# Fourteen rotating weight tiles of an attention and mixer kernel begin 8 to 112 bytes later

## The chip, the cores and the metric

The kernel runs on one core of a Trainium2 chip. The metric is the device time of one execution in microseconds (us), the median of several runs; smaller is better. The engines are named as the profile names them: PE is TensorE (matmul), PEld its weight load, DVE is VectorE, ACT is ScalarE, POOL is GpSimd and SP is SyncE, whose queue carries the DMA transfers here.

## The reference, cut to what matters

```python
def reference(**kwargs):
    attn_out = _attn_ref(q, k, v, n_global, n_local)   # (2, 8, 768, 64)
    x = attn_out.transpose(0, 2, 1, 3).reshape(2, 768, 512)
    # first mixer
    h = np.maximum(x.transpose(0, 2, 1) @ w_tok1, 0.0) @ w_tok2
    u = x + h.transpose(0, 2, 1)
    x = u + np.maximum(u @ w_ch1, 0.0) @ w_ch2         # 512 -> 1536 -> 512
    # second mixer
    theta = x @ w_theta
    zr, zi = x * np.cos(theta), x * np.sin(theta)
    y = np.einsum('ts,bsd->btd', w_tok_r, zr) + np.einsum('ts,bsd->btd', w_tok_i, zi)
    u = x + y
    return u + np.maximum(u @ w_ch, 0.0)
```

Attention keeps a band of 96 keys and 8 global ones. The weights come as float64 and are used in that precision as far as two float32 numbers carry it.

## The kernel before, in words

Each large float32 matmul is split in three: an operand is held as a high and a low part in the type F32R, and `mm3` (line 93) issues high x high, high x low and low x high into one PSUM accumulator. A *split weight tile* holds the high and the low part of a 128 x 512 block: 512 words (2048 bytes) each, one behind the other in each partition, 4096 bytes in all.

The weights are prepared by *jobs*: SP loads the raw 64-bit words into a staging tile `raw`, ACT and DVE and POOL convert them (lines 136 to 146, in tiles `cvt` and `cvs`), then ACT writes the high part into the split weight tile (`job_high`, line 154) and DVE reads it and writes the low part (`job_low`, line 157). A job advances one phase at each `tick`, and ticks stand by hand between the matmuls. No DMA writes a split weight tile.

Where split weight tiles live decides what the change touches:

- Pool `we` has 4 tiles (`EARLY`): the first mixer's channel pieces k = 0 and 1 (two halves each), later `wri0` to `wri3`.
- Pool `ws` has 14 tiles that rotate: the channel pieces of k = 2 to 8 (`wc2_0` to `wc8_1`, made by `channel_piece`), and later, by turns, `wri4` to `wri17` of the second mixer (made by `token`).
- One large tile holds the channel pieces of k = 9 to 11, and later the last weight `wch`; the weight `w_theta` sits in two tiles of the x pool.

A channel piece's half 0 (of `w_ch1`) is the **weight** (stationary) operand of the matmuls `gp<-xh,wc` and `gp<-xl,wc`, 128 words of a part at a time; the moving operand there is the activation. Half 1 (of `w_ch2`) is the **moving** operand of `h<-wc,g`, 512 columns each. The tiles `wri` are the moving operand of `y<-wri,s` and `y<-wri,z`: two of each three with 512 columns, the third (numbers 2, 5, 8, 11, 14, 17) with 256.

The order is written by hand: the attention with the token mixing between (to about 125 us of the span), then `channel_mix`, which for each of the two batches and each k first issues the 24 matmuls of `up` for the next step and then the 18 of `down` for this one, then `PhaseB.run`, which mixes with the 18 `wri` tiles for each batch, then the last matmuls `v`. A value matmul of the attention (line 403) multiplies by 65 columns of a tile `v` or `a`, whose rows lie apart by an odd-looking width:

```python
VW = 2 * D + 2
            po[:, j * OW : j * OW + D + 1], lhsT=at, rhs=v[:, j * (D + 1) : (j + 1) * (D + 1)],
```

With D = 64, block n of such a tile begins 130 n words behind the tile's start, and head j's columns 65 j words further. Every tile of the program begins at a multiple of 32 bytes, and each of the split weight tiles, and of the activations that are matmul operands with them, at 32 bytes past a multiple of 64.

Of the kernel before, what the change touches and what calls it, by code (L numbers as in the profile page):

```python
# [15 lines left out]
F32 = mybir.dt.float32  # L16
# [9 lines left out]
P = 128  # L26
NS = S // P
NHP = H // 2
E = H * D
# [51 lines left out]
class Build:  # L81
# [680 lines left out]
    def token_jobs(self):  # L762
# [16 lines left out]
        for i in range(self.EARLY):  # L779
            self.channel_job(*divmod(i, 2))  # L780

    def channel_piece(self, pool, k, half):
        w = pool.tile([P, 2, E], F32, name="wc%d_%d" % (k, half), tag="w")
        self.set_channel(k, half, w)

    def set_channel(self, k, half, w):
        if half == 0:
# [92 lines left out]
    def moe_jobs(self, ws, w12p):  # L880

        dram = self.dram
        self.start_jobs()
        self.wc_job, self.wr_job = {}, {}
        self.wt, self.wr, self.wch = [], [], []
        self.ws, self.w12p = ws, w12p

        for i in range(2 * NF):
            self.wc_job[divmod(i, 2)] = 0 if i < self.EARLY else self.channel_job(*divmod(i, 2))

        def theta(d):
            if d == 0:
                self.s0 = self.xs.tile([P, NS, E], F32, name="s0", tag="xs")
                self.s1 = self.xs.tile([P, NS, E], F32, name="s1", tag="xs")
                for i in range(NE):
                    t = self.s0 if i < 3 else self.s1
                    j = 2 * (i % 3)
                    self.wt.append((t[:, j], t[:, j + 1]))
            return self.wt[d]

        for d in range(NE):
            self.wt_job = self.add_job(
                dram["w_theta"][d * P : (d + 1) * P, :], lambda d=d: theta(d), 1
            )

        def token(i):
            pool = self.early if i < self.EARLY else ws
            w = pool.tile([P, 2, E], F32, name="wri%d" % i, tag="w")
            self.wr.append((w[:, 0], w[:, 1]))
            return self.wr[i]  # L910

        for i in range(3 * NS):
            s, j = divmod(i, 3)
            self.wr_job[s] = self.add_job(
                dram["w_tok"][s * P : (s + 1) * P, 2 * j * E : 2 * (j + 1) * E],
                lambda i=i: token(i),
                2 + i // 2,
            )

        def last(d):  # L920
            if d == 0:
                w = w12p.tile([P, NS, 2, E], F32, name="wch", tag="w")
                self.wch = [(w[:, i, 0], w[:, i, 1]) for i in range(NE)]
                self.wch_rest = w[:, NE:NS].rearrange("p a l e -> p (a l) e")
            return self.wch[d]

        for d in range(NE):
            self.wch_job = self.add_job(
                dram["w_ch"][d * P : (d + 1) * P, :], lambda d=d: last(d), 1 + NF
            )  # L930
# [354 lines left out]
```

## Time and profile before

| | us |
|---|---|
| median of 3 runs (503.14 to 503.77) | 503.31 |
| the profiled execution, its own time | 503.15 |
| its span, from the first to the last instruction | 501.4 |

| engine | busy us | share of the span | instructions |
|---|---|---|---|
| PE | 495.9 | 99% | 2908 |
| PEld | 421.6 | 84% | 2908 |
| DVE | 309.1 | 62% | 671 |
| ACT | 236.2 | 47% | 458 |
| POOL | 163.4 | 33% | 175 |

A matmul's duration in the profile overlaps that of the next, since matmuls are pipelined. What one costs in a row of them is the distance from its start to the next one's start, called its *step* below. A row of the timeline merges like neighbours (x18) and gives their first start and the time to the last end.

### The profile page before, as it was taken

What the parts mean: (1) busy time and instruction counts of PE and PEld (TensorE: products, weight loads), DVE (VectorE), ACT (ScalarE), POOL (GpSimd) and SP (SyncE); (2) the same over time, 40 slices, a digit from 0 to 9 for tenths busy, and PEclk for the clock granted to TensorE, in tenths of its full rate; (3) what the DMA queues carried; (4) which work ended last, traced back from release to release, by engine and by line L of the source; (5) the groups of instructions that cost most, each with busy time, mean ns of one, the idle gap of its engine ahead of it and who ended that gap; (6) DMA issues with size and microseconds to landing.
All of it is one profiled execution on the core that took longest, in us unless ns stands there. A gap on an engine that the chain in (4) does not pass through costs nothing.

```text
span 501.4 us, 7724 instructions
## 1 busy us (share of the span) xinstructions
PE 495.9 (99%) x2908; PEld 421.6 (84%) x2908; DVE 309.1 (62%) x671; ACT 236.2 (47%) x458; POOL 163.4 (33%) x175
## 2 busy tenths in 40 slices
PE   9999999999999999999999999999999999999997
PEld 4888878887888888888888888888888889888896
DVE  4788878736877575216473565377888886351342
ACT  6888778714755554112554544435555334232010
POOL 7455444410342333001332151144555543333000
PEclk9999999999999999999999999999999999999999
DMA  6797764202453443002443121222210000000012
GB/s 199 209 269 237 227 214 143 85 3 59 152 147 125 135 126 104 0 1 59 118 129 117 42 61 65 85 84 76 73 62 1 1 1 0 22 22 22 21 66 103
DMA packets 30013, 45.93 MB, mean 92 GB/s; under 512 B 1936, under 2 KB 20880, under 8 KB 29968
## 3 DMA queue, kind: packets, MB, share of 16 engines
q1 hardware_dynamic: 29968, 45.36, 29.9%
q8 instruction: 25, 0.41, 0.3%
q14 instruction: 20, 0.16, 0.1%
HBM read 42.21 MB, written 3.15 MB: 90 GB/s over the span
## 4 chain that ended last, share of the span: by engine, by line
PE 98%; ACT 1%; DVE 1%; issue 0%; DVEq 0%; ACTq 0%
PE gp L93 20%; PE y L93 20%; PE h L93 20%; PE th L93 7%; PE v L93 7%; PE o L403 6%; PE mm L93 6%; PE s L434 5%; PE t L481 5%; PE warm L327 1%; PE ut L759 1%; DVE xl L709 0%; ACT xh L703 0%; PE xt_2p L759 0%; PE xt_0p L759 0%; PE xt_1p L759 0%
## 5 line engine op out<-in xcount | busy, mean ns | idle before, releaser
L146 POOL TENSOR_TENSOR cvt<-cvt,cvs 128x512 int32<-128x512 int32 (+1 forms) x57 | 75.8, 1330 | 218.3 <-DVE cvt L145 173.1
L93 PE MATMUL h<-wc,g 128*128 128x512 f32 x432 | 102.5, 391 | 0.0
L93 PE MATMUL gp<-xh,wc 128*128 128x512 f32 (+1 forms) x384 | 98.1, 337 | 0.1
L93 PEld LDWEIGHTS h<-wc,g 128*128 128x128 f32 x432 | 79.7, 188 | 15.7
L705 DVE SCALAR_TENSOR_TENSOR g<-gp,g 128x512 fp32r<-128x512 f32 (+1 forms) x48 | 26.8, 557 | 84.7 <-ACT g L703 84.6
L93 PEld LDWEIGHTS gp<-xh,wc 128*128 128x128 f32 x384 | 67.5, 189 | 8.6 <-DVE xl L709 0.3
L93 PE MATMUL gp<-xl,wc 128*128 128x512 f32 (+1 forms) x192 | 64.5, 336 | 0.0
L703 ACT ACTIVATE g<-gp 128x512 fp32r<-128x512 f32 (+1 forms) x48 | 23.5, 490 | 71.3 <-PE gp L93 71.3
L93 PE MATMUL y<-wri,z 128*128 128x256 f32 (+1 forms) x288 | 52.2, 336 | 0.0
L93 PE MATMUL y<-wri,s 128*128 128x256 f32 (+1 forms) x288 | 52.1, 336 | 0.0
L93 PEld LDWEIGHTS y<-wri,s 128*128 128x128 f32 x288 | 44.9, 190 | 6.0
L93 PEld LDWEIGHTS y<-wri,z 128*128 128x128 f32 x288 | 44.9, 190 | 6.0
L481 PE MATMUL t<-ident,e 128*128 128x128 f32 x176 | 48.1, 285 | 0.4 <-ACT at L493 0.4
L142 DVE SCALAR_TENSOR_TENSOR cvs<-cvt,cvs 128x512 int32<-128x512 int32 (+1 forms) x57 | 44.4, 779 | 0.0
L93 PEld LDWEIGHTS gp<-xl,wc 128*128 128x128 f32 x192 | 36.4, 189 | 4.6
L481 PEld LDWEIGHTS t<-ident,e 128*128 128x128 f32 x176 | 31.6, 184 | 8.2 <-issue 2.3
L136 ACT ACTIVATE cvt<-raw 128x512 f32<-128x512 f32 (+1 forms) x57 | 37.3, 655 | 2.0 <-issue 2.0
L447 DVE CUSTOM_DVE_ANT_0 e<-s,base 128x256 f32<-128x256 f32 (+1 forms) x96 | 32.8, 398 | 8.6 <-PE s L434 8.5
L137 ACT ACTIVATE cvs<-raw 128x512 int32<-128x512 uint16 (+1 forms) x57 | 37.4, 657 | 0.0
L1075 ACT ACTIVATE w<-w 128x512 f32<-128x512 f32 x12 | 7.6, 634 | 57.1 <-DVE w L1072 57.1
L403 PE MATMUL o<-v,at 128*128 128x65 f32 x192 | 32.3, 252 | 0.0
L403 PEld LDWEIGHTS o<-v,at 128*128 128x128 f32 x192 | 29.8, 196 | 0.0
(136 smaller groups left out, 813.9 us busy)
## 6 DMA issues: line engine op xcount, KB each, us to landing
raw<-w_ch SPq DMA_DIRECT2D x28, 512.0 KB, 3.7
raw<-w_tok SPq DMA_DIRECT2D x21, 512.0 KB, 3.6
k<-k SPq DMA_DIRECT2D x7, 480.0 KB, 6.0
v<-v SPq DMA_DIRECT2D x8, 384.0 KB, 3.8
out<-o SPq DMA_DIRECT2D x11, 256.0 KB, 2.0
q<-q SPq DMA_DIRECT2D x7, 384.0 KB, 5.3
raw<-w_theta SPq DMA_DIRECT2D x4, 512.0 KB, 3.7
a<-v SPq DMA_DIRECT2D x8, 240.0 KB, 4.7
```

Of the source, the lines that this page charges most:

```text
L93: self.nc.tensor.matmul(out, lhsT=a, rhs=b, start=first and i == 0, stop=last and i == n - 1)
L136: nc.scalar.activation(out=f(t), in_=f(top), func=AF.Copy, scale=2.0**-111)
L137: nc.scalar.activation(out=s, in_=nxt, func=AF.Copy, scale=2.0**-13)
L142: nc.vector.scalar_tensor_tensor(out=s, in0=t, scalar=-(1 << 31), in1=s, op0=ALU.bitwise_and, op1=ALU.bitwise_or)
L146: nc.gpsimd.tensor_tensor(out=t, in0=t, in1=s, op=ALU.add)
L403: self.nc.tensor.matmul(po[:, j * OW : j * OW + D + 1], lhsT=at, rhs=v[:, j * (D + 1) : (j + 1) * (D + 1)], start=first, stop=last,)
L434: nc.tensor.matmul(ps[j][:, ii, c0:], lhsT=t["q"][pj, i * P : (i + 1) * P], rhs=kf[pj, i * KW - P + c0 : i * KW + P], start=True, stop=True,)
L447: nc.vector.tensor_tensor_reduce(out=e, in0=ps[j][:, ii, c0:], in1=self.base[2 * hp + j][min(i, 1)], op0=ALU.add, op1=ALU.min, scale=-SCAL ...
L481: nc.tensor.transpose(pt[:, ii, c, :], e[j][:, ii, c * P : (c + 1) * P], self.ident)
L703: nc.scalar.activation(out=hi, in_=ps, func=AF.Relu if relu else AF.Copy)
L705: nc.vector.scalar_tensor_tensor(out=lo, in0=ps, scalar=0.0, in1=f(hi), op0=ALU.max, op1=ALU.subtract)
L1075: nc.scalar.activation(out=a, in_=t, func=AF.Abs)
```

## The change

The 14 tiles of pool `ws` grow by 32 words (128 bytes, 4096 to 4224 bytes a tile), and the 4096 bytes of high and low part begin 4, 12, 20, 28, 2, 10 or 6 words behind the tile's start, by turns. For the channel pieces the turn is that of k - 2, so both halves of one k have one offset; for the tiles `wri` it is that of the number less 4. The tiles of `we` and the large tile of k = 9 to 11 keep their places.

```diff
+    SHIFT = (4, 12, 20, 28, 2, 10, 6)
+
+    def split_tile(self, pool, name, n):
+        if pool is self.early:
+            return pool.tile([P, 2, E], F32, name=name, tag="w")
+        w = pool.tile([P, 2 * E + 32], F32, name=name, tag="w")
+        c0 = self.SHIFT[n % len(self.SHIFT)]
+        return w[:, c0 : c0 + 2 * E].rearrange("p (l e) -> p l e", l=2)
+
     def channel_piece(self, pool, k, half):
-        w = pool.tile([P, 2, E], F32, name="wc%d_%d" % (k, half), tag="w")
-        self.set_channel(k, half, w)
+        self.set_channel(k, half, self.split_tile(pool, "wc%d_%d" % (k, half), k - 2))
...
         def token(i):
             pool = self.early if i < self.EARLY else ws
-            w = pool.tile([P, 2, E], F32, name="wri%d" % i, tag="w")
+            w = self.split_tile(pool, "wri%d" % i, i - self.EARLY)
             self.wr.append((w[:, 0], w[:, 1]))
             return self.wr[i]
```

| offset in words | 4 | 12 | 20 | 28 | 2 | 10 | 6 |
|---|---|---|---|---|---|---|---|
| bytes | 16 | 48 | 80 | 112 | 8 | 40 | 24 |
| bytes past a multiple of 32 | 16 | 16 | 16 | 16 | 8 | 8 | 24 |
| channel pieces of k | 2 | 3 | 4 | 5 | 6 | 7 | 8 |
| `wri` | 4, 11 | 5, 12 | 6, 13 | 7, 14 | 8, 15 | 9, 16 | 10, 17 |

On every engine the instructions stand in the order they had, with the shapes and the waits they had. The pool is 14 x 128 = 1792 bytes larger in each partition, so the pools that are placed next to it (`g`, `xt`, `tb`) begin 1792 bytes lower, still at multiples of 32 bytes. All loops, matmuls, copies and transfers are the same in number.

## Rows read from the trace of the kernel before

**Rows 1.** The page: span, busy time by engine, and the chain that ended last.

```profile
span 501.4 us, 7724 instructions
...
PE 495.9 (99%) x2908; PEld 421.6 (84%) x2908; DVE 309.1 (62%) x671; ACT 236.2 (47%) x458; POOL 163.4 (33%) x175
...
PE 98%; ACT 1%; DVE 1%; issue 0%; DVEq 0%; ACTq 0%
```

**Rows 2.** Who PE waited for in the whole span: total us, times, longest.

```profile
PE warm L327 <- DVE halfpi L225: 1.2, 1, 1.2
PE mm L93 <- ACT xh L703: 0.5, 1, 0.5
PE t L481 <- ACT at L493: 0.4, 1, 0.4
```

**Rows 3.** Cores: span and mean granted clock.

```profile
core 0: 501.4 us, clock 1.000
```

**Rows 4.** Tiles wc and wri: count, duration ns min/median/max, first and last start.

```profile
L93 PEld LDWEIGHTS gp<-xh,wc x384: 186/188/192, 125.3 to 324.6; 128*128 128x128 f32 x192
L93 PEld LDWEIGHTS gp<-xl,wc x192: 187/188/192, 125.4 to 324.5; 128*128 128x128 f32 x192
L93 PE MATMUL h<-wc,g x432: 387/389/487, 135.1 to 332.8; 128*128 128x512 f32 x144
L93 PE MATMUL y<-wri,s x288: 277/338/398, 333.0 to 467.1; 128*128 128x256 f32 x72, 128*128 128x512 f32 x72
L93 PE MATMUL y<-wri,z x288: 277/338/398, 344.5 to 478.2; 128*128 128x256 f32 x72, 128*128 128x512 f32 x72
L154 ACT ACTIVATE wc<-cvt x24: 619/632/637, 81.6 to 200.5; 128x512 fp32r<-128x512 f32 x24
L157 DVE SCALAR_TENSOR_TENSOR wc<-cvt,wc x24: 681/682/1740, 84.2 to 202.2; 128x512 fp32r<-128x512 f32 x24
L154 ACT ACTIVATE wri<-cvt x18: 615/626/635, 255.3 to 371.7; 128x512 fp32r<-128x512 f32 x18
L157 DVE SCALAR_TENSOR_TENSOR wri<-cvt,wri x18: 681/684/1153, 260.0 to 381.1; 128x512 fp32r<-128x512 f32 x18
```

**Rows 5.** Timeline of PE in `channel_mix` and `PhaseB`: start us, us, what, count.

```profile
143.39 4.27 PE L93 MATMUL h<-wc,g 128*128 128x512 f32 x18
147.50 0.39 PE L93 MATMUL gp<-xh,wc 128*128 128x512 f32 x1
...
385.16 5.60 PE L93 MATMUL y<-wri,s 128*128 128x512 f32 x24
390.60 3.04 PE L93 MATMUL y<-wri,z 128*128 128x256 f32 x24
393.48 0.60 PE L759 MATMUL xt_2p<-ident,x 128*128 128x128 f32 x4
```

**Rows 6.** Timeline of PE among value matmuls of batch 1, first head pair, blocks 4 and 5.

```profile
60.22 0.33 PE L403 MATMUL o<-v,at 128*128 128x65 f32 x2
60.39 0.28 PE L481 MATMUL t<-ident,e 128*128 128x128 f32 x1
60.50 0.33 PE L403 MATMUL o<-a,at 128*128 128x65 f32 x2
60.67 0.28 PE L481 MATMUL t<-ident,e 128*128 128x128 f32 x1
60.79 0.33 PE L403 MATMUL o<-v,at 128*128 128x65 f32 x2
60.96 0.28 PE L481 MATMUL t<-ident,e 128*128 128x128 f32 x1
61.08 0.34 PE L403 MATMUL o<-a,at 128*128 128x65 f32 x2
61.25 0.28 PE L481 MATMUL t<-ident,e 128*128 128x128 f32 x1
```

**Rows 7.** Timeline of DVE and PE: writes of `wc2_0`, of `wri17`, first read of `wc2_0`.

```profile
130.23 0.68 DVE L157 SCALAR_TENSOR_TENSOR wc<-cvt,wc 128x512 fp32r<-128x512 f32 x1
...
139.24 0.39 PE L93 MATMUL gp<-xh,wc 128*128 128x512 f32 x1
...
381.09 0.68 DVE L157 SCALAR_TENSOR_TENSOR wri<-cvt,wri 128x512 fp32r<-128x512 f32 x1
```

## The prediction

> **What bounds the kernel now.** I read the page first. PE is busy for 495.9 of 501.4 us and the chain that ended last is PE for 98% [rows 1]. Then the waits of PE: three in the whole span, 2.1 us together, none of them for a tile that the change touches [rows 2]. [...] So the time is the sum of the steps of the matmuls, and an edit counts only if it makes a step of PE longer or shorter, or makes PE wait where it doesn't wait now.
>
> The steps come from the timeline. 18 matmuls `h` run from 143.39 to the next one's start at 147.50: 4.11 / 18 = 228 ns for 512 columns. 24 of `y` with 512 columns take 390.60 - 385.16 = 5.44 us, 227 ns each; 24 with 256 columns take 393.48 - 390.60 = 2.88 us, 120 ns each [rows 5]. Between 256 and 512 columns a step grows by 107 ns, so a column costs 107 / 256 = 0.42 ns, and a fixed part of 120 - 107 = 13 ns is left. I use both as prices below.
>
> **The change part by part.** No instruction is added, removed or moved; three kinds of access get a start that is no multiple of 32 bytes.
>
> 1. *Moving reads by PE.* Half 1 of k = 2 to 8 is 7 of 12 channel pieces: 432 x 7 / 12 = 252 matmuls `h` with 512 columns. Of the 576 matmuls `y`, tile numbers 4 to 17 serve: nine tiles with 512 columns, 24 matmuls each, 216; five with 256 columns (5, 8, 11, 14, 17), 48 each, 240 [rows 4]. That is 708 reads on the path, with nothing to hide a longer one.
>
> 2. *Weight loads by PE.* Half 0 of k = 2 to 8: 576 x 7 / 12 = 336 loads [rows 4], half ahead of 512-column matmuls and 168 ahead of 256-column ones. A load lasts 188 ns but lies beside the matmuls before it; a load is behind only where the step is shortest, at 120 ns.
>
> 3. *Writes by ACT and reads and writes by DVE.* 14 channel pieces and 14 `wri` tiles: 28 writes of about 0.63 us on ACT, 28 of 0.68 us on DVE [rows 4]. What hides them is how early they are: the low part of `wc2_0` is done at 130.91 and read at about 139.0, just ahead of the matmul at 139.24; that of `wri17` is done at 381.77 and read by the 256-column run at 390.60 [rows 5, 7]. These are the shortest leads that I found among the 28, 8 us each. If every such write took twice as long, a piece would be late by 1.3 us of its 8. The next instructions on ACT and DVE would be late by that too, the evacuations of `gp` among them, but PE has the whole of a next `up`, 4 us, before it reads their result. So nothing.
>
> 4. *The other tiles.* Pools `g`, `xt` and `tb` slide by 1792 bytes, a multiple of 64, so their starts keep their class. Nothing.
>
> What does a read by PE from such a start cost? No F32R matmul of before has one, so I bound it. The nearest rows are the value matmuls, whose moving operand begins at many places, since a block is 130 words and a head 65. Taken from the code, block 4 of `v` for the first head begins at a multiple of 32 bytes (520 words), block 4 of `a` too, block 5 of `v` 8 bytes past one (650 words), and block 3 of `a` for the second head 28 bytes past one (455 words). Their rows begin at 60.22, 60.50, 60.79 and 61.08, and the next instruction starts 0.17 us later each time [rows 6]. Aligned or not, the same to the 10 ns of the display. That says a start off 32 bytes costs no restart of its own. It leaves one thing open: 260 bytes touch nine 32-byte pieces from any of these starts, and these plain f32 matmuls take their columns more slowly (two instructions and 170 ns for 65 columns). A 2048-byte row touches 64 pieces when it begins on one and 65 when it doesn't.
>
> Bounds: below, nothing, or a gain if the present starts are the slow ones, at most the whole fixed part, 708 x 13 ns = 9.2 us. Above, one 32-byte piece more per moving read, 8 columns x 0.42 = 3.3 ns, 708 x 3.3 = 2.4 us; with one piece in 16 more on the weight loads, 188 / 16 = 12 ns, all of it visible at the 168 short steps, 2.0 us more; at the extreme the fixed part paid twice, +9.2 us. The value matmuls are the nearest row, and by them I take 0.
>
> The rows show 0 for starts of 8 and 28 bytes past a multiple of 32 [rows 6]. [...]
>
> The sum is 0, against the profiled 503.15 us (501.4 of span and 1.75 around it); the median of the runs stands 0.16 above it. I predict 503.3 us. What a measurement of this kernel can tell from no change is about 0.2%, 1.0 us.
>
> **The rivals.**
>
> *One piece more per read (slower).* PE fetches its moving operand in pieces of 32 bytes, and the 65th costs time because PE takes one column after another with no slack. For it: F32R runs at 0.42 ns a column, the engine is busy to 99%, nothing hides a longer read. Against: a buffer ahead of the array would swallow one piece in 65, and rows 6 show no sign of a start that matters. Price 2.4 us, 505.7; with the weight loads 4.4 us, 507.7. It decides from 1.0 us / 708 = 1.4 ns a read, between three and four columns. With pieces of 64 bytes it vanishes, since the starts of before are 32 past a multiple of 64 and each row touches 33 such pieces before and after.
>
> *Small pieces (no change to be seen).* If the pieces are 16 bytes, only the offsets 8, 40 and 24 bytes begin off one: 108 matmuls `h` (k = 6 to 8) and 192 `y` (tiles 8, 9, 10, 15, 16, 17). 300 reads x four columns of 0.42 ns = 0.5 us, 503.8.
>
> *A dear start (slower).* Each off-start read pays its fixed part again: 512.5 us. Against it are the equal steps of the value matmuls [rows 6].
>
> *Late weights (slower).* Writes off 32 bytes are split and get so slow that a piece is late. It begins only when one piece loses more than its 8 us [rows 5, 7], which takes writes of about seven times their length; then several us. I see nothing for it.
>
> *Spread starts (faster).* All split tiles lay 4096 bytes apart; now they are 4224 apart and shifted, so reads by PE and writes by ACT and DVE meet on the same place less often, or the start 32 past 64 was what made the fixed part of 13 ns. For the first: `h` steps 228 where `y` steps 227. That is all there is to win, 1 ns x 432 = 0.4 us, below what can be told. The second would give down to 494.1; nothing in the rows speaks for it.
>
> **How the numbers follow.** Nothing at all 0.62; small pieces 0.08; one piece more 0.17; a dear start 0.05; late weights 0.02; faster by the fixed part 0.06. The first two are within 0.2%, 0.70 in sum, and slower is 0.24. The likeliest case gives 503.3, by itself 502.9 to 503.9. The range goes up over the piece of moving reads (505.7) to 506.0 and down to 502.6; it leaves out the weight loads' extra, the dear start and a real gain, less than 2 in 10.
>
> **What would show it.** Right: `h` for k = 2 to 8 steps as that for k = 9 to 11, which keep their place, 228 ns; `y` 227 and 120 ns; PE's waits still 2.1 us; ACT's and DVE's writes at 0.63 and 0.68 us. One piece more: 231 ns for `h` of k = 2 to 8 alone and 230 and 123 for `y` from tile 4 on. Late weights: a wait of PE for DVE at line 157. Spread starts: steps under 227. The weak point is that the rows for off starts are 65 columns long and not F32R.

## The result and the profile after

The changed kernel takes 506.45 us (median of 5 runs, 506.05 to 506.78) against 503.42 us before; the ratio is 1.006, 95% interval [1.0045, 1.0074]. It is 3.0 us slower, where no change was forecast, and lies 0.45 us above the range.

The page after, its span and busy time by engine:

```profile
span 505.0 us, 7724 instructions
...
PE 498.8 (99%) x2908; PEld 421.4 (83%) x2908; DVE 309.1 (61%) x671; ACT 235.9 (47%) x458; POOL 163.5 (32%) x175
```

PE is busy 2.9 us longer than in [rows 1] with the same instructions; ACT, DVE and POOL are as they were. The profiled execution took 506.78 us, the longest of the five. One wait of PE in it is new against [rows 2]:

```profile
PE s L434 <- DVE x L396: 1.0, 1, 1.0
```

It stands in the attention, at 23.8 us, where no shifted tile is used yet. It lengthens this one execution, whose span is 3.6 us longer while PE is busy 2.9 us longer. Runs below have waits of 0.2 to 1.0 us there too, mostly on transfers, also where nothing is slower; it is no part of the answer. DVE's writes answer [rows 4], the same within 2 ns in the median:

```profile
L157 DVE SCALAR_TENSOR_TENSOR wc<-cvt,wc x24: 680/684/1740, 84.9 to 203.6; 128x512 fp32r<-128x512 f32 x24
```

So it is the steps. Groups of PE by form after (busy us, mean ns):

```profile
L93 PE MATMUL h<-wc,g 128*128 128x512 f32 x432 | 103.9, 394 | 0.0
L93 PE MATMUL gp<-xh,wc 128*128 128x512 f32 x192 | 63.9, 394 | 0.1
L93 PE MATMUL gp<-xh,wc 128*128 128x256 f32 x192 | 38.3, 282 | 0.0
L93 PE MATMUL gp<-xl,wc 128*128 128x512 f32 x96 | 37.6, 391 | 0.0
L93 PE MATMUL y<-wri,z 128*128 128x512 f32 x144 | 34.8, 394 | 0.0
L93 PE MATMUL y<-wri,s 128*128 128x512 f32 x144 | 34.5, 392 | 0.0
```

The same groups of before:

```profile
L93 PE MATMUL h<-wc,g 128*128 128x512 f32 x432 | 102.5, 391 | 0.0
L93 PE MATMUL gp<-xh,wc 128*128 128x512 f32 x192 | 63.3, 390 | 0.1
L93 PE MATMUL gp<-xh,wc 128*128 128x256 f32 x192 | 38.4, 283 | 0.0
L93 PE MATMUL gp<-xl,wc 128*128 128x512 f32 x96 | 37.4, 390 | 0.0
L93 PE MATMUL y<-wri,z 128*128 128x512 f32 x144 | 34.2, 389 | 0.0
L93 PE MATMUL y<-wri,s 128*128 128x512 f32 x144 | 34.0, 389 | 0.0
```

With 512 columns `h` grows by 1.4 us, `gp` by 0.8 and `y` by 1.1: 3.3 us. The 256-column groups shrink a little. Two things fit no price of the prediction: `gp` grows though its moving operand begins where it did, and 256 columns get cheaper. The timeline of PE after shows where `h` grows, 18 matmuls a row for k = 1 (untouched), 2 and 5:

```profile
143.74 4.27 PE L93 MATMUL h<-wc,g 128*128 128x512 f32 x18
...
152.07 4.35 PE L93 MATMUL h<-wc,g 128*128 128x512 f32 x18
...
177.24 4.41 PE L93 MATMUL h<-wc,g 128*128 128x512 f32 x18
```

4.27 us is the row of before [rows 5]. k = 2, at an offset of 16 bytes, and k = 5, at 112, are both multiples of 16 and cost 80 and 140 ns more.

### The profile page after: what moved, and what is told of

Same layout as the page of the kernel before. It is cut to its first block, busy times and chain, and to the rows that moved or that the text cites. A ratio compares the mean times of both kernels' runs of the same rounds, so it can differ in the third digit from the quotient of the medians.

```text
span 505.0 us, 7724 instructions
## 1 busy us (share of the span) xinstructions
PE 498.8 (99%) x2908; PEld 421.4 (83%) x2908; DVE 309.1 (61%) x671; ACT 235.9 (47%) x458; POOL 163.5 (32%) x175
## 4 chain that ended last, share of the span: by engine, by line
PE 97%; DVE 1%; ACT 0%; issue 0%; DVEq 0%; ACTq 0%
PE y L93 20%; PE gp L93 20%; PE h L93 20%; PE th L93 7%; PE v L93 7%; PE o L403 6%; PE mm L93 6%; PE s L434 5%; PE t L481 5%; PE warm L327 1%; PE ut L759 1%; DVE xl L709 0%; PE xt_1p L759 0%; PE xt_2p L759 0%; PE xt_0p L759 0%
## 5 line engine op out<-in xcount | busy, mean ns | idle before, releaser
L93 PE MATMUL h<-wc,g 128*128 128x512 f32 x432 | 103.9, 394 | 0.0
```

The source lines that it names most:

```text
L93: self.nc.tensor.matmul(out, lhsT=a, rhs=b, start=first and i == 0, stop=last and i == n - 1)
```

## The experiments

Two theories at first. **A**: a read by PE from a start off 32 bytes has a cost of its own. **B**: the step depends on how the moving operand and the weights loaded beside it lie to one another. The rival **C** is the padding: the tiles are 4224 bytes apart, and other pools lie lower.

**The padding alone, and other offsets.** The edit in the first two is the list of offsets (words):

```diff
-    SHIFT = (4, 12, 20, 28, 2, 10, 6)
+    SHIFT = (0, 0, 0, 0, 0, 0, 0)         # pad_only
+    SHIFT = (8, 16, 24, 32, 8, 24, 16)    # mult32
```

> The 14 tiles are 4224 bytes long, but their contents begin at the tile's start. Theory A (each read by PE from a start off 32 bytes has a cost of its own) and theory B (a weight load and the moving read beside it disturb one another, by how their starts lie to each other) both expect the time of before, 503.4 us, with gp at 227 ns a step for 512 columns and h at 228. Theory C (the larger distance between tiles or the lower places of g, xt and tb do it) expects the time of the change, 506.4 us.

> As the change, but the seven offsets are 32, 64, 96, 128, 32, 96 and 64 bytes, all multiples of 32. Theory A expects 503.4 us. Theory B expects 503.4 us if the starts matter to one another only within 32 bytes; if over a longer period (64 or 128 bytes), between 504 and 506.5 us, with gp and h steps of 230 ns and more for those k whose offset differs from that of the other operand.

Measured: 505.77 us for the padding alone, a ratio of 1.0051 [1.0034, 1.0068] to before, and 506.01 us for multiples of 32 bytes, 1.0056 [1.004, 1.0073]. The padding alone, with every start a multiple of 32 bytes, costs 2.4 of the 3.0 us. A falls as the main cause, and so does B with a period of 32 bytes, which expected 503.4 us too. When I predicted, I had thought of the padding only as a gain, in *Spread starts*. The remaining 0.6 us is not clear of noise by the times alone: the interval of the change, [1.0045, 1.0074], overlaps that of the padding. PE's timeline with the padding alone, `h` for k = 1, 2 and 7:

```profile
143.75 4.27 PE L93 MATMUL h<-wc,g 128*128 128x512 f32 x18
...
152.01 4.35 PE L93 MATMUL h<-wc,g 128*128 128x512 f32 x18
...
193.84 4.35 PE L93 MATMUL h<-wc,g 128*128 128x512 f32 x18
```

In the first batch k = 2 to 7 cost 4.35 each, k = 1 4.27. Where the tiles lie gives theory **D**: the step depends on the distance between the starts of the weights and of the moving operand, modulo 256 bytes. Before, all operands of the F32R matmuls begin at 224 past a multiple of 256 bytes. A pitch of 4224 = 16.5 x 256 puts every second tile 128 bytes off that. Those are the tiles `wc*_1`, which `h` reads, and half of `wri`; the tiles `wc*_0` keep their distance, and `gp` for k = 3 keeps its 227 ns a step (`gp` for k = 4 to 8, each behind an `h` run that is out of step, takes 228 to 229). A matmul also suffers from its neighbours: after the change `gp` of k = 9 and 10, whose operands kept their places, steps at 231 and 229 ns behind `h` runs that step at 236 and 233, where before both stepped at 227. In the run with multiples of 32, k = 5 has an offset of 128 bytes, which undoes the padding, and its `h` alone is near 4.27 again (k = 4 and 5):

```profile
168.69 4.36 PE L93 MATMUL h<-wc,g 128*128 128x512 f32 x18
...
177.10 4.31 PE L93 MATMUL h<-wc,g 128*128 128x512 f32 x18
```

**Weights alone, moving operands alone.** Here `split_tile` gives the offset only to half 0, or only to the rest.

```diff
-        c0 = self.SHIFT[n % len(self.SHIFT)]
+        c0 = self.SHIFT[n % len(self.SHIFT)] if name.startswith("wc") and name.endswith("_0") else 0
```

> Only half 0 of the channel pieces is shifted, which PE reads as weights; all moving operands begin where they did. Theory A in the form of the prediction (only moving reads pay) expects 503.4 us and gp at 227 ns. Theory B expects the gp part of the loss alone: 512-column gp steps of k = 3 to 8 at 231 to 233 ns, 256-column ones at 117 to 119 ns, h of k = 2 to 8 back at 228 ns; about +0.8 us, 504.2 us.

> Only what PE reads as moving operand is shifted: half 1 of the channel pieces and wri. Theory A: h steps of k = 2 to 8 and y steps as in the change, gp back at 227 ns: +2.3 us, 505.7 us. Theory B: the same size, +2.3 us, 505.7 us, but with gp of k = 2 to 9 back at 227 ns only some matmuls after an h run has ended out of step. With the run that shifts the weights alone it tells whether the two parts add up to 3.0 us.

Measured: 505.82 us, 1.0053 [1.0036, 1.007], and 506.35 us, 1.0066 [1.0049, 1.0082]. All the expected times (503.4 and 504.2 us, then 505.7) left out the padding, which both runs carry, and so the parts do not add up; as a split of the loss they decide nothing. What they do show: with the weights alone shifted, `gp` with 512 columns goes to 63.8 + 37.7 us, near the change's 63.9 + 37.6, from 63.4 + 37.5 with the padding alone. For k = 3, whose `gp` the padding leaves at 227 ns, it steps at 233.

**The distances restored.** The padding stays, the contents of the odd tiles begin 128 bytes in:

```diff
+    ODD = ["wc%d_1" % k for k in range(2, 9)] + ["wri%d" % i for i in (6, 8, 10, 12, 14, 16, 17)]
...
-        c0 = self.SHIFT[n % len(self.SHIFT)]
+        c0 = 32 if name in self.ODD else 0
```

> Tiles of 4224 bytes as in the change, but the contents begin 0 or 128 bytes in, whichever makes all of them lie a multiple of 4096 / 16 = 256 bytes from one another and from the other operands, as before. Theory D (a step depends on the distance between the start of the weights being loaded and the start of the moving operand beside them, modulo 256 bytes; at distance 0 it settles at 227 ns) expects the time of before, 503.4 us, with h at 228 ns for every k and gp at 227. Theory C (the pitch of 4224 bytes or the lower places of g, xt and tb, whatever the distances) expects 505.8 us as with the padding alone.

Measured: 503.51 us, 0.9994 [0.998, 1.0008]. `h` for k = 7, at the same pitch of 4224 bytes; k = 2 to 6 read alike:

```profile
193.41 4.27 PE L93 MATMUL h<-wc,g 128*128 128x512 f32 x18
```

C falls: neither the pitch nor the lower pools cost anything when the distances are right. Some of the distances here are odd multiples of 256 bytes, so a multiple of 512 is not needed.

**Place or distance.** Without the change: the tiles of the left side 64 bytes lower, then those of the right side too.

```diff
-            cp.tile([P, 32], F32, name="shim")
+            cp.tile([P, 16], F32, name="shim")      # left64, all64
...
+            es.enter_context(tc.tile_pool(name="sr", bufs=1, side="right")).tile([P, 16], F32, name="shim_r")      # all64
```

> The kernel before with one tile of 128 bytes at the front of the memory made 64 bytes: all tiles on the left side (x, xh, xl, the z tiles, w_theta) begin 64 bytes lower, those on the right (weights wc, wri, g, xt) stay; every start is still a multiple of 32 bytes. Theory D: operands that meet across the sides (gp, y) leave step, 512 columns at 230 to 234 ns, and h, whose two operands both lie on the right, stays at 228 but for some matmuls after a gp run; 505 to 507 us. Theory A (only a start off 32 bytes pays) expects 503.4 us.

> As the run with the left side 64 bytes lower, and the right side lowered by 64 bytes too: every start changes, no distance between operands does. Theory D expects 503.4 us and the steps of before. Theory E (what counts is the place of each start by itself, such as 224 past a multiple of 256) expects at least the loss of the run with the left side alone, 505 to 507 us or more.

Measured: 505.14 us, 1.0026 [1.0011, 1.0041], and 503.48 us, 0.9992 [0.9977, 1.0008]. Moving one side costs, moving both doesn't: E falls, the distance counts. The groups with only the left side moved:

```profile
L93 PE MATMUL h<-wc,g 128*128 128x512 f32 x432 | 102.3, 390 | 0.0
L93 PE MATMUL gp<-xh,wc 128*128 128x512 f32 x192 | 64.3, 395 | 0.1
L93 PE MATMUL gp<-xl,wc 128*128 128x512 f32 x96 | 37.8, 394 | 0.0
L93 PE MATMUL gp<-xh,wc 128*128 128x256 f32 x192 | 37.0, 278 | 0.0
```

`h`, with both operands on the right, stays; `gp`, across the sides, gets dearer with 512 columns and cheaper with 256 (395 and 278 ns in the mean where before they lasted 390 and 283), and so does `y` (393 to 394 and 279 ns against 389 and 283).

**The price by itself.** A program of 40 matmuls a series on fixed operands. It computes none of the reference's work.

```diff
+                    for j in range(self.REPS):
+                        nc.tensor.matmul(
+                            t, lhsT=r(wgt[:, w0 : w0 + P]), rhs=r(mov[:, m0 : m0 + n]),
+                            start=j == 0, stop=j == self.REPS - 1,
+                        )
```

> Does none of the reference's work and writes zeros and some sums: 46 series of 40 F32R matmuls each, always the same two operands, with 512 or 256 columns. The moving operand begins 0 to 240 bytes past the place of the weights modulo 256, in steps of 16 bytes; in six more series both begin 8, 16, 24, 32, 64 and 128 bytes later. Theory D: 227 ns (512 columns) and 120 ns (256 columns) at distance 0 and in all series where both move together, starts off 32 bytes among them; other distances settle elsewhere, most of them at 230 to 236 ns for 512 columns, some at 113 to 118 for 256. Theory A: series with a moving start off 32 bytes are slower than those on 32 bytes by some 3 to 6 ns, whatever the weights' start, also where both move together by 8, 16 or 24 bytes.

PE's timeline; a step is the distance to the next row's start over 40. The rows `tma` to `tmc` are distances 0, 16 and 32, `tmp` is 240; in `tbotha` to `tbothd` both operands begin 8, 16, 24 and 32 bytes later:

```profile
25.29 9.23 PE L106 MATMUL tma<-mov,wgt 128*128 128x512 f32 x40
34.36 9.43 PE L106 MATMUL tmb<-mov,wgt 128*128 128x512 f32 x40
43.62 9.50 PE L106 MATMUL tmc<-mov,wgt 128*128 128x512 f32 x40
52.96 9.49 PE L106 MATMUL tmd<-mov,wgt 128*128 128x512 f32 x40
...
164.55 9.24 PE L106 MATMUL tmp<-mov,wgt 128*128 128x512 f32 x40
173.63 9.40 PE L106 MATMUL tbotha<-mov,wgt 128*128 128x512 f32 x40
182.87 9.37 PE L106 MATMUL tbothb<-mov,wgt 128*128 128x512 f32 x40
192.07 9.50 PE L106 MATMUL tbothc<-mov,wgt 128*128 128x512 f32 x40
201.41 9.26 PE L106 MATMUL tbothd<-mov,wgt 128*128 128x512 f32 x40
210.51 9.25 PE L106 MATMUL tbothe<-mov,wgt 128*128 128x512 f32 x40
```

Distance 0 steps at 227 ns (9.07 / 40) and so does 240; 16 and 32 at 232 and 234, and all others of the 16 distances at 229 to 235. D holds as long as both starts are multiples of 32: moved together by 32 bytes the series stays at 227 to 228 ns (9.10 us for 40). Moved by 8, 16 or 24 it does not, against D, and takes 231, 230 and 233 ns. But A does not hold either: at distance 240 the moving operand begins 16 bytes past a multiple of 32, and the step is 227. With 256 columns the order is another one; distances 0, 112 and 192:

```profile
228.71 4.96 PE L106 MATMUL tha<-mov,wgt 128*128 128x256 f32 x40
233.51 4.92 PE L106 MATMUL thb<-mov,wgt 128*128 128x256 f32 x40
...
261.95 4.72 PE L106 MATMUL thh<-mov,wgt 128*128 128x256 f32 x40
266.51 4.90 PE L106 MATMUL thi<-mov,wgt 128*128 128x256 f32 x40
...
285.45 4.72 PE L106 MATMUL thm<-mov,wgt 128*128 128x256 f32 x40
290.01 4.93 PE L106 MATMUL thn<-mov,wgt 128*128 128x256 f32 x40
```

Here 0 is of the dearest sort, 120 ns, and 112 and 192 cost 114.

**More of it by itself.** The same program with other starts, narrower weights, and bf16.

```diff
+        for cols, what in ((P, "full"), (64, "half"), (32, "quarter")):
+            for d in (0, 16):
+                out.append((what + "xy"[d // 16], 512, d, 0, cols))
+        for d in (0, 16, 4):
+            out.append(("bf" + "xyz"[(0, 16, 4).index(d)], 512, 2 * d, 0, -P))
```

> Does none of the reference's work, as the first series. 512 columns throughout, 40 matmuls a series: moving starts at 8, 24, ... 248 bytes' distance; moving starts at 0 to 240 bytes with the weights 16 bytes later; weights of 128, 64 and 32 columns at distance 0 and 64; the same in bf16 at distance 0, 64 and 16. Theory D: most off-32 distances at 229 to 236 ns, with 227 again for weights 16 later and moving at 0. If the fixed part of 13 ns is the reading of the weights beside the moving operand, it falls with their columns: about 220 ns with 64 and 217 with 32 columns, and the loss at distance 64 shrinks likewise; bf16 stays near 216 ns at any distance, having half the bytes to read. If the fixed part belongs to the matmul itself, fewer weight columns change nothing.

In `twsixteenf` the weights begin 16 bytes later and the moving operand 64 bytes past them:

```profile
221.39 9.24 PE L117 MATMUL twsixteenf<-mov,wgt 128*128 128x512 f32 x40
230.46 9.36 PE L117 MATMUL twsixteeng<-mov,wgt 128*128 128x512 f32 x40
...
322.71 9.23 PE L117 MATMUL tfullx<-mov,wgt 128*128 128x512 f32 x40
331.77 9.34 PE L117 MATMUL tfully<-mov,wgt 128*128 128x512 f32 x40
340.95 9.37 PE L117 MATMUL thalfx<-mov,wgt 128*64 128x512 f32 x40
350.15 9.30 PE L117 MATMUL thalfy<-mov,wgt 128*64 128x512 f32 x40
359.29 9.42 PE L117 MATMUL tquarterx<-mov,wgt 128*32 128x512 f32 x40
368.55 9.44 PE L117 MATMUL tquartery<-mov,wgt 128*32 128x512 f32 x40
377.83 8.81 PE L117 MATMUL tbfx<-mbf,wbf 128*128 128x512 bf16 x40
386.47 8.80 PE L117 MATMUL tbfy<-mbf,wbf 128*128 128x512 bf16 x40
395.10 8.79 PE L117 MATMUL tbfz<-mbf,wbf 128*128 128x512 bf16 x40
```

bf16 steps at 216 ns at distances 0 and 64, and its third row is as long. Narrower weights don't shrink the fixed part: at distances 0 and 64 full weights take 227 and 229 ns, half of the columns 230 and 228, a quarter 231 and 232. My guess that the fixed part is the reading of the weights fell. The 16 odd distances (8, 24, ... 248 bytes) took 230 to 236 ns; with the weights 16 bytes later three of 16 moving starts took 227 and three more 228. One of them is distance 64, 9.07 / 40 = 227 ns, where weights at a multiple of 32 take 229. So off the multiples of 32 the distance alone doesn't set the step.

**The offsets without the padding's part.** The distances restored, and the seven offsets on those contents that need no 128 bytes for it, half of them.

```diff
-        c0 = self.SHIFT[n % len(self.SHIFT)]
+        c0 = 32 if name in self.ODD else self.SHIFT[n % len(self.SHIFT)]
```

> As the run that restores all distances modulo 256 bytes, but the seven tiles of k = 2 to 8, half 0, and wri 4, 5, 7, 9, 11, 13 and 15, which need no 128 bytes for that, get the change's seven offsets of 8 to 112 bytes. This prices the offsets without the padding's part. Theory D with the steps of the timed series: gp of k = 3 to 8 at 231 to 234 ns for 512 columns and 117 to 119 for 256, +0.7 us; the y matmuls of the five shifted 512-column tiles at 231 to 234 ns, +0.5 us, their partners somewhat; the two 256-column tiles at 118 to 119 ns, -0.1 us; together 504.6 to 505.3 us. Theory C (the padding does all): 503.5 us.

Measured: 504.81 us against 503.23, 1.0026 [1.0017, 1.0035], as expected of D (A would expect a loss here too). So the offsets, which are themselves distances, cost too when the others are right: 1.6 us by the medians on half of the tiles, 0.9 to 1.8 by the interval. In the change they add 0.6 us. That they fall there largely on matmuls that the padding has already put out of step would explain it, but no run shows this by itself.

**A faster version.** Distance 0, or weights 16 bytes later, for 512 columns; 112 and 192 for the 256-column tiles.

```diff
-        c0 = self.SHIFT[n % len(self.SHIFT)]
+        c0 = self.START.get(name, 32 if name in self.ODD else 4 if name.endswith("_0") else 0)
...
+    START = {"wri5": 28, "wri11": 28, "wri8": 16, "wri14": 16, "wri17": 16}
```

> All 512-column operands at distance 0 modulo 256 bytes, or with the weights 16 bytes later (half 0, distance 240), which the timed series show to settle at 227 ns too and at 117 instead of 120 ns with 256 columns; the 256-column tiles wri 5 and 11 at distance 112 and 8, 14 and 17 at distance 192, which settle at 113 ns in the series. Theory D: 5 x 48 x 6.7 ns = 1.6 us less in y and 7 x 24 x 2 ns = 0.3 us less in gp: 501.6 us. Theory A (starts off 32 bytes cost) expects no gain: 503.5 us or more.

Measured: 502.65 us, 0.9985 [0.9976, 0.9994] against 503.23. It beats both kernels, the one before by 0.6 us where 1.9 were expected. Many of its operands begin off 32 bytes, which A takes for a loss. The timeline of the 256-column `y` runs with tiles 11, 14 and 17:

```profile
367.26 2.92 PE L93 MATMUL y<-wri,z 128*128 128x256 f32 x24
...
378.63 2.99 PE L93 MATMUL y<-wri,s 128*128 128x256 f32 x24
...
390.10 3.29 PE L93 MATMUL y<-wri,z 128*128 128x256 f32 x24
```

Against 3.04 us [rows 5] tile 11 gains, 14 a little, and 17 loses, where all should have come to about 2.9. In the run with multiples of 32 bytes the run of tile 17, with the same two places, took 2.89:

```profile
393.16 2.89 PE L93 MATMUL y<-wri,z 128*128 128x256 f32 x24
```

So one pair of starts can settle in more than one way. `gp` of k = 7 with 512 columns shows it too: at the same two starts it steps at 233 ns after the change and at 227 in the run with the offsets on half of the tiles. And `h` of k = 5 after the change lies at distance 240, where the series steps at 227; it takes 236. What decides it is open.

## Why the prediction was wrong, point by point

**The bound** was right: PE's steps are the time, and the change acted through them alone.

**The step that failed** is the list of what the edit touches: "three kinds of access get a start that is no multiple of 32 bytes." It judged each start by itself, by its place within 32 or 64 bytes, and the sum has no term for the other thing that the edit does: the pitch of 4224 bytes moves every second of the 14 tiles by 128 bytes against the operands that they meet in a matmul. That was put at nothing without a reason; only *Spread starts* names the pitch, as a gain of at most 0.4 us. The padding alone costs 2.4 us, and with the distances modulo 256 bytes restored, nothing. The fourth part was right in what it said of the pools that slide: 1792 is 7 x 256, and the run with the distances restored has them at their lower places.

**The price of a moving read** was sought in the read itself. The 0 from the value matmuls [rows 6] was carried from plain f32, 65 columns in two instructions, to F32R, 512 columns in one; the series moved together by 8 to 24 bytes show 3 to 7 ns for F32R. That is the second failure, and the smaller one: 3.0 - 2.4 = 0.6 us of the change by the medians, though 1.6 us on half of the tiles where the distances were right. And the price is not that of a read: it belongs to the two starts together, since the series at distance 240 reads off 32 bytes at 227 ns.

**The weight loads** were called behind only at the 256-column steps. They are the other way round: with the weights alone shifted, `gp` of k = 3 steps at 233 ns with 512 columns where the padding alone leaves 227, and with 256 columns at 118 instead of 119.

**The writes** were rightly priced at nothing: they last as long as before (684 ns in the median on DVE against 682, 631 on ACT against 632), and PE has no wait for them.

**The rivals.** *One piece more per read* gave 505.7 us, near the measured time, and its sign, 231 ns for `h` of k = 2 to 8 alone, nearly came (231 to 236 in the first batch). That is luck: its mechanism needs reads off 32 bytes, and the padding alone, which has none, gives 233. *Small pieces* falls too: `h` takes 4.35 and 4.41 us at offsets of 16 and 112 bytes, 4.38 and 4.40 at 8 and 40. No run shows pieces of 16, 32 or 64 bytes; the runs show a price of the distance between two starts, also where both are multiples of 32. *A dear start* would have given 512.5 us, and *late weights* a wait of PE that isn't there. *Spread starts* had the right object, how the operands lie to one another, and the wrong sign. I dismissed the sign of it that the rows had: `h` at 228 where `y` steps at 227. In the trace of before the first five steps of an `h` run right behind 256-column matmuls are 229 to 235 ns and the rest 226 to 227: it falls into step. With the padding alone the 18 steps of k = 3 take 233 ns in the mean, and after the change those of k = 2 stay at 233 to 236 from the sixth to the last.

For bf16 the series show no price of a distance: 216 ns at 0 and at 64. For F32R 16 bytes are not free even where both operands move together: that series takes 230 ns instead of 227.

What stays open is the mechanism below the steps: why 256 bytes, why most starts off 32 bytes settle badly and some do not, why the same two starts settle in two ways, and what the fixed part of 13 ns is, since narrower weights do not lessen it.

## What to carry to other kernels

A pad of a tile is not free because it is small: it changes how operands that meet in a matmul lie to one another, and cost 2.4 us here. For F32R matmuls with 512 columns keep the moving operand and the weights a multiple of 256 bytes apart, each at a multiple of 32: in the three kernels here whose operands all do so, and in the series, the steps took 227 to 228 ns in the mean. A pitch of 4096 bytes does it, one of 4224 doesn't. When a layout edit moves a time by half a per cent, run it with the same layout and unshifted contents before explaining the shift.

## What the runs showed of the hardware that I had not expected

- F32R matmuls settle into a rhythm: after the change `gp` of k = 9, whose operands kept their places, steps at 224 to 236 ns ten times and at 227 from the eleventh. Series of 40 on unchanged operands, the weights at a multiple of 32, take 227 ns a step with 512 columns at distances 0 and 240 and 229 to 236 at the others; with 256 columns 120 ns at distance 0, 114 at 112 and 192. bf16 takes 216 at distances 0 and 64.
- Distance 0, the cheapest for 512 columns, is of the dearest sort for 256. So a round of `up` and `down` changes little when its `gp` operands shift: with the left side 64 bytes lower the 512-column `gp` matmuls cost more (395 ns in the mean against 390) and the 256-column ones less (278 against 283), and from one `h` run's start to the next it takes 8.27 us, against 8.26 before. Distance 240 is better for both in the series: 227 and 117 ns.
